# Batch 0 of a Fourier mixing layer: turning rows to partitions with VectorE transposes in SBUF in place of a trip through HBM

## The chip, the cores and the metric

One core of one Trainium2 chip runs the whole kernel. The metric is device time in microseconds (us), lower is better. Engines are named as in the profile: PE is TensorE's matmuls, PEld its weight loads, DVE is VectorE, ACT ScalarE, POOL GpSimd, SP SyncE (it only issues DMAs here). "L291" is a line of the kernel that was profiled, so one statement has different numbers in different kernels.

Ratios below are the mean time of one kernel's fast runs over the mean time of the other's fast runs of the same rounds on the same chip, with a 95% interval. They are therefore not quite the ratio of the medians that stand beside them.

## The reference, cut to what matters

```python
X = np.fft.rfft(x, axis=1)                  # x: 8 x 3008 x 256
y = np.fft.irfft(X * F, n=3008, axis=1)     # F = filt_r + 1j * filt_i
out = (np.maximum(y @ w_gate, 0) * (y @ w_val)) @ w_out    # 24064 rows, 256 -> 1536 -> 256
```

## The kernel before

The transform of length 3008 is done as 94 x 32, all in matmuls:

- **Stage A** transforms along the 94 (`n1`, on the partitions). Its output has the frequency rows on the partitions and the 32 values of `n2` in the free direction.
- **Stage B** needs `n2` on the partitions: it transforms along `n2`, multiplies with the filter, and transforms back.
- **The inverse** along the 94 gives `yT`, and the **main loop** does the gate, value and output matmuls over 47 blocks of 512 rows.

Batch 0 does the first three steps alone, as a prologue. Batch 1's stage A is spread over batch 0's stage B, the later batches over the main loop. Before the change batch 0's data were turned by writing stage A's rows to HBM and reading them back in another order:

```python
Abuf = [dram.tile([NROW * N2, D], BF16, name=f"Abuf{b}") for b in range(B)]
...
def items_a(b):                              # 16 items; 4 of them make a chunk c
    def one(c, j, st):
        ...
        nc.tensor.matmul(psA[0:NROW], WA, XF[c * NC2 // NX2][:, o:o + 512], start=True, stop=True)
        nc.scalar.copy(dst, psA[0:NROW])
        if j == 3:                           # chunk c complete: write it
            eng = nc.scalar if b and c > 1 else nc.sync
            eng.dma_start(_ap(Abuf[b], ...), st["asb"][:NROW])
...
def load_at(b, c):                           # ... and read it with n2 on the partitions
    nc.sync.dma_start(ats[b][c:c + 125:4], _ap(Abuf[b], c * NROW * NC2 * D, [[D, 32], [4 * NC2 * D, NG], [1, D]]))
```

The prologue, cut:

```python
warm(11)                                     # junk matmuls
for i, f in enumerate(items_a(0)): f()       # stage A of batch 0
for c in range(4): load_at(0, c)
... make_back_t, make_back_u (tables), place_filter (copies of the filters), place_nyq
for i in range(14): warm(2)                  # junk matmuls during the trip
load_x(1, nc.sync, ...)                      # x of batch 1
early = items_a(1)
def amid(i):                                 # called in step i of stage B
    if i < 2: warm(6, 256)
    else:
        for _ in range((1, 1, 2, 1, 1)[i - 2]): next(early)()
first_b(amid)                                # stage B of batch 0, six steps
load_d(0, 0, 2)                              # stage B's output goes through HBM too (Dbuf -> dC)
...
load_at(1, 0)
for i, f in enumerate(early):                # the rest of batch 1's stage A
    f()
    if i == 5: load_at(1, 1)
    if i == 7:
        for h in range(2): item_c(0, h)      # first inverse, then the main loop starts
```

## Time and profile before

| | before |
|---|---|
| median of three runs | 894.28 us |
| span of the profiled run | 892.0 us |
| first product of stage B starts (VectorE) | 34.78 us |
| stage B's last output copy ends (ScalarE) | 51.00 us |
| first inverse matmul starts | 57.35 us |
| first value matmul of the main loop starts | 59.59 us |
| longest idle time of TensorE between stage A and the main loop | 2.14 us (32.20 to 34.34) |

Most of the lines from which this comes stand in the prediction below. The four points in time in the middle are the ones to follow: from the last of them on TensorE is full (busy for 825.09 of the 832 us from 60 us on in the kernel before), so what that point moves, the end moves. Two more lines of the kernel before will be compared, the stretches around the start of the main loop (columns: length; busy us of PE, PEld, DVE, ACT, POOL with the number of instructions; granted clock of TensorE; DMA share; GB/s):

```profile
55.00:60.00 5.00, 4.54 (x23) 1.83 (x22) 0.69 (x1) 3.12 (x6) 4.04 (x7) 1.00 1.09 195
60.00:65.00 5.00, 4.64 (x21) 1.94 (x20) 2.70 (x5) 3.20 (x6) 5.00 (x4) 1.00 1.20 272
```

The column to note is the clock, 1.00 in both.

### The profile page before, as it was taken

To read this page: it belongs to the slowest core of one execution; us is meant where nothing else is said; L and a number is where in the kernel's file an instruction comes from. 1 tells how busy PE (TensorE), PEld (TensorE's weight loads), DVE (VectorE), ACT (ScalarE), POOL (GpSimd) and SP (SyncE) were. 2 spreads that over 40 slices of the span, in tenths; PEclk is the share of its full clock that TensorE was granted. 3 is DMA by queue.
4 is the path that set the end of the run, shared out by engine and by line. 5 is a ranking of instruction groups with operands and counts; after the bars stand their busy time and mean duration, and the time that the engine had idled before them with its cause. 6 is when DMAs were issued, how large, how long until landed. Compare 5 with 4: busy or idle time off the path is not lost.

```text
span 892.0 us, 19155 instructions
## 1 busy us (share of the span) xinstructions
PE 875.7 (98%) x7208; PEld 506.8 (57%) x7208; DVE 567.1 (64%) x871; ACT 504.2 (57%) x893; POOL 364.4 (41%) x361
## 2 busy tenths in 40 slices
PE   7899999999999999999999999999999999999997
PEld 2335655566556665566655565556655566666665
DVE  2736776577665766667766677657776577655553
ACT  4675555555655566556555556555655555555553
POOL 4350697038651476316671176802867000000001
PEclk9999999999999999999999999999999999999999
DMA  9997448534456336453376334662446512331111
GB/s 244 305 235 141 143 138 166 119 102 130 120 142 133 116 97 155 130 125 97 96 174 146 86 102 109 175 139 78 116 141 148 121 31 81 76 79 36 37 32 53
DMA packets 114099, 109.18 MB, mean 122 GB/s; under 512 B 20359, under 2 KB 98599, under 8 KB 113366
## 3 DMA queue, kind: packets, MB, share of 16 engines
q1 hardware_dynamic: 90294, 80.10, 34.7%
q0 software_dynamic: 22992, 26.41, 12.3%
q8 instruction: 57, 0.93, 0.5%
q10 hardware_dynamic: 720, 1.45, 0.4%
q14 instruction: 36, 0.29, 0.1%
HBM read 61.93 MB, written 49.81 MB: 125 GB/s over the span
## 4 chain that ended last, share of the span: by engine, by line
PE 93%; DMA 3%; ACT 1%; POOL 1%; issue 1%; DVE 0%; SPq 0%; ACTq 0%; POOLq 0%
PE psV L467 28%; PE psG L467 27%; PE psO L486 27%; PE psF L323 3%; PE psY L451 2%; PE psD L394 2%; PE psX L364 2%; PE psA L276 2%; DMA dC<-Dbuf 1%; DMA Abuf<-asb 1%; DMA at<-Abuf 1%; DMA XF<-in_x_dram 1%; ACT dsb L401 0%; DMA Dbuf<-dsb 0%; SPq L176 0%
## 5 line engine op out<-in xcount | busy, mean ns | idle before, releaser
L472 DVE SCALAR_TENSOR_TENSOR prod<-psG,vsb 128x512 bf16<-128x512 f32 x564 | 389.2, 690 | 263.6 <-ACT vsb L470 258.1
L470 ACT CAST vsb<-psV 128x512 bf16<-128x512 f32 x564 | 331.8, 589 | 263.0 <-PE psV L467 170.9
L467 PE MATMUL psV<-yT,WvT 128*128 128x512 bf16 x1128 | 336.6, 380 | 0.7 <-ACT asb L330 0.4
L486 PE MATMUL psO<-WoT,prod 128*128 128x256 bf16 x2256 | 336.5, 273 | 0.0
L467 PE MATMUL psG<-yT,WgT 128*128 128x512 bf16 x1128 | 335.4, 379 | 0.7 <-ACT dsb L401 0.3
L486 PEld LDWEIGHTS <-prod 128*128 128x128 bf16 x2256 | 220.2, 98 | 143.8
L467 PEld LDWEIGHTS <-WgT 128*128 128x128 bf16 x1128 | 109.9, 97 | 135.9 <-issue 2.5
L467 PEld LDWEIGHTS <-WvT 128*128 128x128 bf16 x1128 | 98.4, 98 | 41.9 <-issue 30.4
L258 POOL CAST scr<-prod 128x8 f32<-128x8 bf16 x24 | 4.5, 189 | 258.3 <-DVE prod L472 258.3
L509 POOL DMA_DIRECT2D out_dram<-osb x5 | 2.6, 536 | 195.9 <-ACT osb L499 195.9
L499 ACT COPY osb<-psO 128x512 f32<-128x512 f32 x92 | 53.9, 586 | 27.6 <-PE psO L486 26.1
L380 DVE TENSOR_TENSOR tt<-psX,Ftr 128x512 bf16<-128x512 f32 x96 | 65.1, 682 | 5.9 <-PE psX L364 5.9
L309 POOL TENSOR_TENSOR fold<-XP 128x1024 f32<-128x1024 f32 x24 | 56.5, 2355 | 20.5 <-PE psF L323 19.2
L380 DVE TENSOR_TENSOR uu<-psX,Fti 128x512 bf16<-128x512 f32 x89 | 60.6, 681 | 0.0
L401 ACT CAST dsb<-psD 128x512 bf16<-128x512 f32 x96 | 51.5, 589 | 12.1 <-PE psD L394 11.8
L296 POOL DMA_DIRECT2D XP<-in_x_dram x96 | 56.7, 596 | 3.2 <-PE psG L467 1.6
L310 POOL TENSOR_TENSOR XP<-XP 128x1024 f32<-128x1024 f32 x24 | 56.4, 2349 | 1.9
L330 ACT CAST asb<-psF 128x512 bf16<-128x512 f32 x48 | 25.8, 589 | 30.5 <-PE psF L323 30.5
L330 DVE CAST asb<-psF 128x512 bf16<-128x512 f32 x48 | 30.9, 686 | 18.6 <-PE psF L323 18.6
L456 ACT CAST yT<-psY 128x512 bf16<-128x512 f32 x47 | 27.5, 586 | 23.8 <-PE psY L451 23.6
L451 PE MATMUL psY<-M,dC 96*128 96x94 bf16 (+18 forms) x604 | 37.7, 199 | 1.4 <-DMA dC<-Dbuf 1.2
L458 DVE CAST yT<-psY 128x512 bf16<-128x512 f32 x47 | 32.0, 681 | 9.8 <-PE psY L451 9.8
(72 smaller groups left out, 493.5 us busy)
## 6 DMA issues: line engine op xcount, KB each, us to landing
at<-Abuf SPq DMA_DIRECT2D x32, 384.0 KB
dC<-Dbuf SPq DMA_DIRECT2D x64, 192.0 KB
XP<-in_x_dram POOLq DMA_DIRECT2D x48, 256.0 KB, 6.1
Dbuf<-dsb SPq DMA_DIRECT2D x23, 512.0 KB
XP<-in_x_dram POOLq DMA_DIRECT2D x96, 96.0 KB, 2.7
Abuf<-asb SPq DMA_DIRECT2D x96, 96.0 KB
out_dram<-osb SPq DMA_DIRECT2D x69, 94.0 KB
XF<-in_x_dram SPq DMA_DIRECT2D x15, 256.0 KB
```

Of the source, the lines that this page charges most:

```text
L296: nc.gpsimd.dma_start(xp[r:r + 24, 0:4:2, :], _ap(x, (b * N1 * N2 + o) * D, [[N2 * D, 24], [47 * N2 * D, 2], [1, 512]]))
L309: tt(t, xp[:, 0:2], xp[:, 2:4], op=ALU.add)
L310: tt(xp[:, 2:4], xp[:, 0:2], xp[:, 2:4], op=ALU.subtract)
L330: copy(asf[:, :, q, :], banks[q])
L380: nc.vector.tensor_tensor(p, psX, filt, op=ALU.mult)
L401: nc.scalar.copy(dsb[:, a, o:o + 2, :], psD[a])
L451: nc.tensor.matmul(psY[:, o:o + w], dCs[b, n2 // 8][:, n2 % 8, h * 128:(h + 1) * 128], M1[:, n1:n1 + w], start=True, stop=True)
L467: nc.tensor.matmul(pt[:, :W], w[:, h, ft * 128:(ft + 1) * 128], yt[:, h, :], start=(h == 0), stop=(h == 1))
L470: nc.scalar.copy(vsb, psV[:, :W])
L472: nc.vector.scalar_tensor_tensor(prod, in0=psG[:, :W], scalar=0.0, in1=vsb, op0=ALU.max, op1=ALU.mult)
L486: nc.tensor.matmul(psO[:, t % 2], prods[ft][:, t * 128:(t + 1) * 128], WoT[:, ft, :], start=(ft == 0), stop=(ft == NFT - 1))
L499: copy(osb[:, t0 % 2:t % 2 + 1], psO[:, t0 % 2:t % 2 + 1])
```

## The change

Its intent is to take the write and the read through HBM off the start of the kernel. Stage A of batch 0 now computes 128 rows in an order of their own, ScalarE writes them as bf16 into `AS`, and two VectorE transposes, to which pairs of bf16 are given as one 4-byte word, turn `AS` into `AT`, which stage B reads. Around this the prologue is rearranged. The diff, cut to its core:

```diff
-    wa = np.zeros((128, NROW))
+    wa = np.zeros((128, 128 + NROW))          # a second set of columns, in the turn's order
...
+    AS = pro.tile([128, NC2, N2 // NC2, D], BF16)
+    AT = pro.tile([128, 32, D], BF16)
...
+    def first_a(i):
+        c, j = divmod(i, 4)
+        psA = matmul_a(c, j, slice(0, 128))
+        nc.scalar.copy(AS[:, 2 * j:2 * j + 2, c, :], psA.rearrange("p (n d) -> p n d", n=2))
+    def turn_a():
+        src = AS.rearrange("p l c d -> p (l c) d").bitcast(FP32).rearrange("p n d -> p d n")
+        dst = AT.bitcast(FP32).rearrange("p k d -> p d k")
+        for h in range(2):
+            cols = slice(h * D // 4, (h + 1) * D // 4)
+            nc.vector.transpose(dst[:, cols, :], src[:, cols, :])
+        ats[0] = AT
...                                            # prologue; the tables now come ahead of stage A
-    for i, f in enumerate(items_a(0)):
-        f()
-    for c in range(4):
-        load_at(0, c)
+    for i in range(16):
+        first_a(i)
...
+    for a in range(2):
+        place_filter(0, a, 0, nc.vector.tensor_copy)
+    turn_a()
+    for i in range(9):                         # was 14, and warm(6)
+        warm(2)
...                                            # upper filter halves by DMA, x of batch 1 behind them
+            place_filter(fi, a, 1, nc.sync.dma_start)
+        load_x(1, nc.sync, cols)
...
     def amid(i):
-        if i < 2:
-            warm(6, 256)
-        else:
-            for _ in range((1, 1, 2, 1, 1)[i - 2]):
-                next(early)()
+        if i == 3:
+            place_nyq()
+        for _ in range((1, 1, 1, 2, 1, 2, 1)[i]):
+            next(early)()
...
     for i, f in enumerate(early):
         f()
-        if i == 5:
+        if i == 2:
             load_at(1, 1)
-        if i == 7:
+        if i == 4:
             for h in range(2):
                 item_c(0, h)
```

So 9 instead of 6 of batch 1's stage-A items lie inside stage B, and 5 instead of 8 between stage B and the first inverse.

More of the change, by code (lines that the diff above doesn't have):

```diff
@@ L57, in _tables @@
         e, j = g % 2, 12 * a + g // 2
-        ra, rm = 4 * j + 2 * e, 48 * e + j
+        rt, ra, rm = 64 * e + j, 128 + 4 * j + 2 * e, 48 * e + j
         f = np.zeros((64, 64))
@@ L63, in _tables @@
         th = 2 * np.pi * (((n1 - 23) * k1) % N1) / N1
-        wa[part, ra] = np.cos(th)
+        wa[part, rt] = wa[part, ra] = np.cos(th)
         if k1 not in (0, 47):
-            wa[part, ra + 1] = -np.sin(th)
+            wa[part, rt + 32] = wa[part, ra + 1] = -np.sin(th)
             m1[rm] = 2.0 * np.cos(th) / S
@@ L152 @@
     pro = prologue.enter_context(tc.tile_pool(name="pro", bufs=1))
-    Abuf = [dram.tile([NROW * N2, D], BF16, name=f"Abuf{b}") for b in range(B)]
+    Abuf = [dram.tile([NROW * N2, D], BF16, name=f"Abuf{b}") if b else None for b in range(B)]
     Dbuf = [dram.tile([NROW * N2, D], BF16, name=f"Dbuf{b}") for b in range(B)]
     XF = [pro.tile([128, NX2 * D], FP32, name=f"XF{c}") for c in range(N2 // NX2)]
-    WA = pro.tile([128, NROW], FP32)
+    WA = pro.tile([128, 128 + NROW], FP32)
+    AS = pro.tile([128, NC2, N2 // NC2, D], BF16)
+    AT = pro.tile([128, 32, D], BF16)
     WF = consts.tile([128, 4, 32], FP32)
@@ L267, in fft_tag, with matmul_a @@
         return turn["tags"][turn["i"] % len(turn["tags"])]
+    def matmul_a(c, j, cols):
+        psA = ps.tile([128, 512], FP32, tag=fft_tag(True), name="psA")
+        o = (c * NC2 % NX2) * D + j * 512
+        nc.tensor.matmul(psA[0:cols.stop - cols.start], WA[:, cols], XF[c * NC2 // NX2][:, o:o + 512],
+                         start=True, stop=True)
+        return psA
+    def first_a(i):
[9 more added lines that the diff above has]
+        ats[0] = AT
     def items_a(b):
@@ L273, in one @@
                 st["asb"] = sb.tile([128, NC2 * D], BF16, tag="asb", bufs=4, name="asb")
-            psA = ps.tile([128, 512], FP32, tag=fft_tag(True), name="psA")
-            o = (c * NC2 % NX2) * D + j * 512
-            nc.tensor.matmul(psA[0:NROW], WA, XF[c * NC2 // NX2][:, o:o + 512],
-                             start=True, stop=True)
-            dst = st["asb"][:NROW, j * 512:(j + 1) * 512]
-            nc.scalar.copy(dst, psA[0:NROW])
+            psA = matmul_a(c, j, slice(128, 128 + NROW))
+            nc.scalar.copy(st["asb"][:NROW, j * 512:(j + 1) * 512], psA[0:NROW])
             if j == 3:
-                eng = nc.scalar if b and c > 1 else nc.sync
+                eng = nc.scalar if c > 1 else nc.sync
                 eng.dma_start(_ap(Abuf[b], c * NROW * NC2 * D, [[NC2 * D, NROW], [1, NC2 * D]]),
@@ L541 @@
         pass
-    warm(11)
-    for i, f in enumerate(items_a(0)):
-        f()
-    for c in range(4):
-        load_at(0, c)
+    warm(8)
     for i in range(3):
         make_back_t(i)
-    warm(6)
-    place_filter(0, 1, 0, nc.scalar.copy)
-    for i in range(3):
-        make_back_u(i)
-    for a, half in ((0, 0), (0, 1), (1, 1)):
-        place_filter(0, a, half, nc.vector.tensor_copy)
-    place_own()
-    for a, half, copy in ((1, 0, nc.scalar.copy), (0, 0, nc.vector.tensor_copy),
-                          (0, 1, nc.vector.tensor_copy), (1, 1, nc.vector.tensor_copy)):
-        place_filter(1, a, half, copy)
-    place_nyq()
-    for i in range(14):
-        warm(2)
-    load_x(1, nc.sync, ((0, 0, 2 * q), (0, 2 * q, 4 * q), (1, 0, 4 * q)))
+    warm(3)
+    for i in range(16):
+        first_a(i)
+        if i == 3:
+            for n in range(3):
+                make_back_u(n)
+    place_own()
+    for a in range(2):
+        place_filter(0, a, 0, nc.vector.tensor_copy)
+    turn_a()
+    for i in range(9):
+        warm(2)
+    place_filter(1, 1, 0, nc.scalar.copy)
+    place_filter(1, 0, 0, nc.vector.tensor_copy)
+    for fi, cols in ((0, ((0, 0, 2 * q), (0, 2 * q, 4 * q))), (1, ((1, 0, 4 * q),))):
+        for a in range(2):
+            place_filter(fi, a, 1, nc.sync.dma_start)
+        load_x(1, nc.sync, cols)
     nc.sync.dma_start(WF, nc.inline_tensor(fold_h, name="dft_fold").ap())
@@ L568, in amid @@
     def amid(i):
-        if i < 2:
-            warm(6, 256)
-        else:
-            for _ in range((1, 1, 2, 1, 1)[i - 2]):
-                next(early)()
-    hold_gpsimd(ats[0][0:32, NG - 1, 0:8])
+        if i == 3:
+            place_nyq()
+        for _ in range((1, 1, 1, 2, 1, 2, 1)[i]):
+            next(early)()
+    hold_gpsimd(AT[0:32, NG - 1, D - 8:])
     load_vg(0, DFF // 2)
@@ L580 @@
     load_d(0, 0, 2)
-    nc.gpsimd.dma_start(pro.tile([1, D], BF16, tag="last", bufs=1, name="last"),
+    nc.gpsimd.dma_start(pro.tile([1, D], BF16, tag="nyq", bufs=2, name="last"),
                         _ap(Dbuf[0], (N2 * NROW - 1) * D, [[D, 1], [1, D]]))
```

## The prediction

> **What bounds the kernel now.** I read the page first (busy shares, then the chain that ended last), then the busy time by stretches of the span, then the chain in order of time over the first 60 us, and last the groups of instructions and the waits of that stretch.
>
> ```profile
> span 892.0 us, 19155 instructions
> PE 875.7 (98%) x7208; PEld 506.8 (57%) x7208; DVE 567.1 (64%) x871; ACT 504.2 (57%) x893; POOL 364.4 (41%) x361
> PE 93%; DMA 3%; ACT 1%; POOL 1%; issue 1%; DVE 0%; SPq 0%; ACTq 0%; POOLq 0%
> ...
> 200.00:400.00 200.00, 200.00 (x1720) 116.89 (x1719) 133.99 (x206) 114.66 (x206) 104.18 (x97) 1.00 0.50 128
> ...
> 30.00:35.00 5.00, 2.86 (x22) 1.25 (x20) 2.44 (x6) 2.00 (x1) 0.33 (x2) 1.00 0.98 317
> ```
>
> The columns of the stretches are length, then busy time of PE, PEld, DVE, ACT, POOL, the granted clock, the DMA share and GB/s. From 60 us on TensorE has work without a gap (200.00 of 200 us): nothing done for batch 0 can shorten that part. It can only start earlier. So the change is worth exactly what it moves the first gate/value matmul of the main loop, at 59.6 us. The head of the chain, in order of time (start, length, what):
>
> ```profile
> 12.82 10.53 PE psA L276 x24
> 23.35 0.02 issue
> 23.37 0.59 ACT asb L279
> 23.96 0.02 issue
> 23.98 5.43 DMA Abuf<-asb
> 29.41 0.02 issue
> 29.42 0.02 SPq L350
> 29.44 0.03 issue
> 29.47 4.78 DMA at<-Abuf
> 34.25 0.09 issue
> 34.34 0.46 PE psX L364 x8
> 34.80 0.67 DVE tt L380
> ...
> 51.03 2.41 DMA Dbuf<-dsb
> ...
> 53.83 3.39 DMA dC<-Dbuf
> 57.21 0.14 issue
> 57.35 0.62 PE psY L451 x12
> ```
>
> The reader is to see a turn of the data through HBM: stage A ends on TensorE at 23.35, ScalarE's last copy at 23.96, then a write of 5.43 us and a read of 4.78 us, and only at 34.34 the first stage-B matmul. That is 10.4 us from copy to matmul in which TensorE does table making and warm-up matmuls on junk. After it comes the stage B of batch 0 (34.80 to 51.03), a second trip through HBM (51.03 to 57.21), and the main loop.
>
> [...]
>
> **The change part by part.**
>
> Stage A itself: the same 16 products of 128 rows by 512 columns, now with 128 instead of 96 output rows. The records of one item are two matmuls, 24 of them in 10.53 us, 0.439 us each; [...] The table of weights grows from 48 to 112 KB and is loaded first: at 241 GB/s (stretch 5 to 10 us) an estimated 0.2 to 0.3 us on the arrival of x, which sets the 12.82. The table making (48 small matmuls, three swaps) moves ahead of and into stage A. Its data (384 and 135 KB on ScalarE's queue) are all moved by 6 us, and TensorE waits for x until 12.82 with only 8 records' work (3.9 us) to do; 0.74 us of small matmuls and 0.9 us of swaps fit. End of stage A's copies: 23.96 + 0.25 = 24.2.
>
> The turn: two VectorE instructions, each 128 partitions x 64 x 32 fp32 words = 2048 elements. The pace is from two rows of groups, VectorE casts from fp32:
>
> ```profile
> L197 DVE CAST I2t<-psI 128x256 bf16<-128x256 f32 x6 | 2.1, 416 | 17.3 <-PE psI L192 17.3
> L458 DVE CAST yT<-psY 128x512 bf16<-128x512 f32 x1 | 0.7, 691 | 9.3 <-PE psY L451 9.3
> L238 DVE COPY Ftr<-Ftr 32x3072 bf16<-32x3072 bf16 x3 | 2.8, 948 | 0.1
> ```
>
> The medians are 414 and 681 ns, so 267 ns for 256 elements, 1.04 ns an element, and 147 ns fixed. 2048 x 1.04 + 147 = 2.28 us each, 4.6 us both (an estimate). Ahead of them VectorE copies two filter halves (2 x 0.95 us); the r filters land at about 22 in the trace before (last issued at 14.41, longest landing 7.5 us) and somewhat earlier without stage A's writes in the way, so these copies are over by 24. The turn ends at 24.2 + 4.6 = 28.8. Stage B's first matmuls need 0.46 us, but VectorE still has one filter copy (0.95) before the first product: product at 29.8 against 34.80 before. Gain 5.0 us. All of it is on the path; of the 10.4 us of DMA about half comes back as VectorE time.
>
> The upper filter halves: before, six VectorE copies and two of ScalarE; now three and one, and four DMAs of 192 KB inside SBUF. They are needed at the earliest at the fourth of six steps of stage B, some 8 us after its start, so they are hidden. ScalarE's 2.75 us copy of the i filter starts when that filter has landed. Before it waited until 29.25; with 0.43, 0.23 and 0.37 MB of stage A's writes gone from the stretches 16 to 25 us, I put it at 27, end 29.8, just in time for the first product with the i filter at 30.4.
>
> Stage B: the warm-up matmuls of steps 0 and 1 become stage-A items of batch 1, and there are 9 items inside it instead of 6. Each is one more ScalarE copy of 0.58 us. ScalarE is what is full there:
>
> ```profile
> 40.00:45.00 5.00, 4.28 (x54) 2.01 (x54) 3.66 (x6) 4.71 (x11) 4.16 (x4) 1.00 1.06 238
> 45.00:50.00 5.00, 5.00 (x64) 2.05 (x63) 2.60 (x5) 4.78 (x11) 1.16 (x1) 1.00 0.86 279
> ```
>
> Followed copy by copy: the two early ones push the first output copy (39.09 before, 4.29 us after the first product) by 0.6 us, later steps carry some 0.25 more, and the third extra one adds 0.58, of which 0.3 fits into ScalarE's gaps. Stage B gets 1.1 us longer.
>
> After stage B: 5 items of batch 1 instead of 8 lie before the first matmul of the inverse. They cover the second trip through HBM, which needs 6.3 us and doesn't get shorter; TensorE then idles about 3 us, at no cost. Two items stay after it, as before. One more 0.38 MB write of batch 1 falls next to the last writes of stage B: 0.4 us (an estimate, a third of the 1.2 us that it takes at 317 GB/s).
>
> Sum: -5.0 + 1.1 + 0.4 = -3.5 us; 894.3 - 3.5 = **890.8 us**.
>
> **The rivals.**
>
> First: the transposes run at half pace because of the 512-byte steps. Then they take 2 x (147 + 4096 x 1.04) = 8.8 us, the start gains 0.8 only, and stage B's extra work makes it 895. [...] Against: the diff cuts the warm-up matmuls ahead of stage B from 34 to 18 (0.22 us each). Before, they end at 32.2, 2.1 us ahead of the first stage-B matmul; now they end at 27.4. Whoever tuned this expected stage B at about 29.5.
>
> Second: the filters become the wait that takes the place of the trip through HBM. The DMA engines are full from 10 to 45 us (share 0.96 and more), and x of batch 1 is now requested at about 22 instead of 30, right among the i filter's packets. If that filter still lands at 29.2, ScalarE's copy ends at 32.0 and the first product with it comes 1.6 us late: 892.4. For it: the saturated DMA. Against: 3 MB less of A's traffic in the same time.
>
> Third: ScalarE or the first item's x doesn't delay stage B at all, since its copies find gaps. Then only the start counts: 889.3 with the 0.4, and 888.9 without.
>
> Fourth: the weights hold the main loop, so an earlier start is hidden. Their first halves are asked for at 34.84 and take up to 11.8 us, far ahead of 59.6; now they are asked for at 29. The second halves are asked for after stage B's last write and shift with it. I see no wait for them in TensorE's list (largest after 24 us: 2.1 for the turned data). This one would make 894; I hardly believe it.
>
> **Range and chances.** 80% goes to 888.8 to 893.8: the lower end is the third rival, the upper end is the second with a slow start of x or some part of the first. About 12% lies above (half pace), the rest below. The most that the removed trip could give is 10.4 us, 1.2%, so faster than 2% (under 876.4) can't come from here, and no part costs the 18 us for slower. Within 2%: 0.98.
>
> **What would show it right or wrong.** Right: two transposes of 2.2 to 2.4 us each starting near 24.2, the first stage-B matmul near 28.9, the first product near 29.8, the last stage-B output copy near 47, the first gate/value matmul near 56, and TensorE full from there as before. Half pace shows as 4.4 us transposes; the second rival as ScalarE's filter copy starting after 28 on a DMA and VectorE or TensorE waiting behind it; the third as a stage B of 16.2 us; the fourth as a TensorE wait for weights after 56. Wrong altogether would be a stage A that ends a microsecond or more later, because the table making ahead of it holds up its first items, or a wait for x of batch 1 in stage B's first steps.

What is cut, with a mark, are general statements on the hardware: a paragraph on transposes, SBUF and DMAs, a clause on stage A, and one ground for the first rival. The sum: it came to -5.0 + 1.1 + 0.4 = -3.5 us, so 890.8. Stage A's wider output counts as zero in it, which was the author's estimate (measured since: in the chains 24 records in 10.55 us with 128 rows, 10.53 with 96). The pace of the transposes was an estimate from two casts, and the "half pace" of the first rival a supposition that no trace showed then.

## More of the kernel before

The rounds ran on different chips, and the kernel before has medians between 893.51 and 895.19 us in them. A fall of the time that is reckoned from one round to another is uncertain by as much; the points in time in the traces are the surer measure.

## The result, and the profile after

The changed kernel is correct and slower: 900.11 us (899.61 to 900.52, 4 runs) against 894.16 us, ratio 1.0068, interval 1.0051 to 1.0086. Within the class "within 2%" that had been given 98%, but outside the range, and of the wrong sign.

| | before | after | difference |
|---|---|---|---|
| first product of stage B starts | 34.78 | 32.48 | -2.30 |
| stage B, first product to end of last output copy | 16.22 | 17.77 | +1.55 |
| second trip through HBM, from there to the first inverse matmul | 6.35 | 10.81 | +4.46 |
| from there to the first value matmul | 2.24 | 4.37 | +2.13 |
| first value matmul starts | 59.59 | 65.43 | +5.84 |

The differences of the first four rows add up to the last one, and the last is nearly the whole difference of the medians, 5.95. The lines of the last row, before and after:

```profile
59.59 0.60 PE L467 MATMUL psV<-yT,WvT 128*128 128x512 bf16 x2
65.43 1.06 PE L488 MATMUL psV<-yT,WvT 128*128 128x512 bf16 x2
```

The four rows can be taken one by one. The chain that ended last, of the changed kernel, in order of time:

```profile
22.59 0.59 ACT AS L283
...
23.35 3.93 issue
27.27 4.19 DVE AT L291
...
50.28 2.42 DMA Dbuf<-dsb
...
53.22 7.80 DMA dC<-Dbuf
...
61.06 1.03 PE psY L472 x12
62.10 3.54 PE psA L275 x4
65.64 0.85 PE psV L488 x2
```

The reader is to see four things. The trip of 10.2 us is gone, but the turn takes its place with 8.3 us (the first transpose is shown as "issue", 23.35 to 27.27, and the second by name). The read of the second trip, `dC<-Dbuf`, takes 7.80 us where it took 3.39. And the same matmuls after it are slow: 12 inverse matmuls 1.03 us instead of 0.62, the first value pair 0.85. The group of the transposes (count, busy us, mean ns of one, idle time before them):

```profile
L291 DVE STREAM_TRANSPOSE AT<-AS 128x2048 f32<-128x2048 f32 x2 | 8.3, 4225 | 2.1 <-ACT AS L283 2.1
```

4.2 us for 2048 words, where 2.28 had been predicted. What TensorE waited for, longest first (total, times, longest), and the stretches of the changed kernel that match the slow places:

```profile
PE psY L472 <- DMA dC<-Dbuf: 7.5, 1, 7.5
PE psX L385 <- DVE AT L291: 5.1, 1, 5.1
```

```profile
30.00:35.00 5.00, 3.48 (x19) 1.16 (x20) 4.58 (x6) 0.60 (x2) 2.37 (x3) 0.50 0.96 314
55.00:60.00 5.00, 0.00 (x0) 0.00 (x0) 0.00 (x0) 0.00 (x0) 1.76 (x3) 0.72 0.99 178
60.00:65.00 5.00, 3.94 (x16) 1.96 (x17) 0.69 (x1) 1.17 (x2) 1.80 (x3) 0.50 1.21 254
```

After each of the two waits the clock column falls to half: 0.50 from 30 to 35 us and from 60 to 65 us, where the kernel before has 1.00. That was nowhere in the prediction.

The theory after this reading has four parts: the transposes are slow because of their 512-byte steps; the idle time of TensorE during the turn costs clock in stage B; batch 1's third stage-A write, which the denser schedule puts 0.35 us ahead of the `dC` reads, holds these reads; and the long wait that follows costs clock again. Rivals: a 4-byte transpose is slow as such; stage B is longer because ScalarE has more to copy; the `dC` reads are slow because of the weights or of the earlier `load_at(1, 1)`; the slow start of the main loop is a matter of data, not of clock.

### The profile page after: what moved, and what is told of

It reads as the page before. It is cut to its first block, busy times and chain, and to the rows that moved or that the text cites. A ratio compares the mean times of both kernels' runs of the same rounds, so it can differ in the third digit from the quotient of the medians.

```text
span 898.4 us, 18964 instructions
## 1 busy us (share of the span) xinstructions
PE 868.5 (97%) x7059; PEld 507.2 (56%) x7180; DVE 573.3 (64%) x870; ACT 501.9 (56%) x892; POOL 365.6 (41%) x361
## 3 DMA queue, kind: packets, MB, share of 16 engines
HBM read 60.42 MB, written 48.23 MB: 121 GB/s over the span
## 4 chain that ended last, share of the span: by engine, by line
PE 85%; DVE 5%; ACT 4%; DMA 3%; issue 2%; SPq 1%; POOL 1%; DVEq 0%; ACTq 0%
PE psG L488 26%; PE psO L507 25%; PE psV L488 24%; DVE prod L493 3%; ACT vsb L491 3%; PE psF L344 3%; PE psD L415 2%; DMA dC<-Dbuf 2%; PE psA L275 2%; PE psX L385 2%; PE psY L472 2%; SPq L178 1%; DVE AT L291 0%; DMA XF<-in_x_dram 0%; POOL uu L399 0%
## 5 line engine op out<-in xcount | busy, mean ns | idle before, releaser
L488 PE MATMUL psG<-yT,WgT 128*128 128x512 bf16 x1107 | 331.0, 379 | 6.7 <-DVE prod L493 0.5
L488 PE MATMUL psV<-yT,WvT 128*128 128x512 bf16 x1030 | 315.9, 380 | 0.5 <-ACT asb L351 0.5
```

The costliest lines, as they stand in the source:

```text
L488: nc.tensor.matmul(pt[:, :W], w[:, h, ft * 128:(ft + 1) * 128], yt[:, h, :], start=(h == 0), stop=(h == 1))
```

## The experiments

Twelve kernels ran. All edits are to the changed kernel unless said otherwise. This is where each has its four points (us), with the median, the kernel before in the same rounds, and the ratio:

| kernel | first product | stage B ends | first inverse | first value | median | before | ratio (95%) |
|---|---|---|---|---|---|---|---|
| e1_fill_turn | 32.22 | 49.31 | 60.01 | 64.13 | 899.07 | 895.19 | 1.0045 (1.0025 to 1.0065) |
| e2_fill_trip | 32.63 | 50.43 | 61.38 | 63.63 | 897.24 | 895.19 | 1.0028 (1.0012 to 1.0043) |
| e3_late_write | 32.37 | 49.64 | 56.21 | 60.55 | 894.67 | 895.19 | 1.0003 (0.9987 to 1.0018) |
| e5_fewer_items | 32.57 | 47.96 | 54.52 | 56.76 | 892.28 | 893.51 | 0.9987 (0.9971 to 1.0004) |
| c1_three | 32.48 | 49.56 | 56.22 | 58.46 | 894.22 | 893.51 | 1.0008 (0.9990 to 1.0025) |
| c4_few_fill | 32.84 | 48.23 | 54.63 | 56.88 | 891.95 | 894.23 | 0.9969 (0.9954 to 0.9983) |
| c2_sliced | 28.36 | 44.30 | 50.78 | 53.02 | 888.19 | 893.51 | 0.9940 (0.9920 to 0.9961) |
| c3_no_x_wait | 27.65 | 43.42 | 49.63 | 51.88 | 888.19 | 894.25 | 0.9939 (0.9924 to 0.9955) |

### The clock after the turn: e1_fill_turn

```diff
     turn_a()
-    for i in range(9):
+    for i in range(17):
         warm(2)
```

> The changed kernel with 34 instead of 18 junk matmuls during the turn, so that TensorE doesn't idle 5.1 us before stage B. If the idle gap is what halved the granted clock (0.50 at 30 to 35 us), the clock stays near 1.0 there, the first two stage-A items inside stage B take 1.1 instead of 2.0 us, stage B from its first product to its last output copy goes from 17.8 to some 16.8 us, and the time falls by about 1 us to 899. If stage B is longer only because of the extra items on ScalarE, it stays at 17.8 and the time at 900.1.

The idle time before stage B shrank from 5.08 to 1.62 us and the clock stayed up, as the stretch of this kernel shows:

```profile
30.00:35.00 5.00, 3.48 (x33) 1.15 (x34) 4.94 (x7) 0.86 (x2) 2.56 (x4) 1.00 0.94 316
```

Stage B took 17.09 us instead of 17.77, the first value matmul came 1.3 us earlier, and the median is 1 us lower. So in these two traces the clock costs stage B 0.7 us; the other 0.9 of its 1.55 are not clock, and both theories get a part. The 0.7 is not a fixed price. In e3_late_write the same gap (5.11 us) was followed by half clock until about 34.8 us, where the changed kernel has it until about 36.7, and stage B took 17.27 us.

### The clock after the second trip: e2_fill_trip

```diff
         if i == 4:
+            for _ in range(16):
+                warm(2)
             for h in range(2):
                 item_c(0, h)
```

> The changed kernel with 32 junk matmuls in the gap of 7.5 us that TensorE idles before the first inverse matmul. If that gap costs clock (0.63 at 60 to 70 us), the stretch from the first inverse matmul to the first value matmul goes from 4.6 back to 2.4 us and the time falls by 2.5 to 3 us, to 897.3. If the slow start of the main loop is a matter of DMA or weights, the time stays at 900.1.

In the chain of this kernel the inverse (0.62 in the kernel before) and the two items after it (1.78, as in the kernel before) are back to their old lengths:

```profile
61.38 0.64 PE psY L472 x12
```

From the first inverse to the first value matmul it is 2.25 us instead of 4.37, though the `dC` data land as late as before the edit. The slow start of the main loop is the clock: it is 1.00 from 60 to 65 us here, 0.50 in the changed kernel. The median fell by 2.9 us, as expected, the profiled run by 2.3 and the first value matmul by 1.8.

### The late read of the second trip: e3_late_write and e5_fewer_items

```diff
-                eng = nc.scalar if c > 1 else nc.sync
+                eng = nc.scalar if c > 2 else nc.sync      # e3_late_write: the third write queues behind the reads
```

> The changed kernel with the third write of batch 1's stage A put on the queue behind the reads of the second trip instead of on ScalarE's queue ahead of them. If that write is what held the reads (2 us in which their queue moved 0.02 MB), the reads land 3.5 to 4 us after their first issue instead of 7.8, the gap of TensorE shrinks to about 4 us, and the time falls by 3.5 to 5 us, to 895 to 896.6. If the reads are slow because of the weights or of the re-read of batch 1's rows, they still take over 7 us and the time stays at 900.

DMA traffic from 53 to 55 us by queue (packets, MB, share of the 16 engines). First the changed kernel, where q10 is ScalarE's queue with the write and q1 SyncE's with the reads, then e3_late_write:

```profile
q10 hardware_dynamic: 95, 0.36, 78.8%
q1 hardware_dynamic: 36, 0.02, 3.0%
```

```profile
q1 hardware_dynamic: 840, 0.42, 84.3%
```

In the changed kernel the write has the engines for most of these 2 us and the reads move 0.02 MB; the weights then come on (queue q0) while the reads are still at it. Without the write ahead of them the reads land after 3.35 us instead of 7.80, though `load_at(1, 1)` is issued at 55.60, no later than in the changed kernel (56.34), so that rival falls.

The write itself accounts for about 1 us of this, as a finer cut of the same traces shows. Where no write stands ahead of them, the reads move their first packets some 0.9 us after their first issue (issued at 53.45 and moving from about 54.4 in the kernel before, 52.35 and 53.3 in e3_late_write). In the changed kernel it is 1.9 us (52.85 and 54.8): from 53.75 to 54.75 us the write's queue moved 0.18 MB and the queue of the reads nothing. The rest comes from what the reads meet when they are late. In e3_late_write they have 84.3% of the engines' time from 53 to 55 us and land at 56.07. In the changed kernel they have moved 0.22 MB by 56 us, against 0.57 in e3_late_write, and from 56 to 61 us the weights take 66% of the engines' time. The weights alone are not the cause, since e3_late_write has them as well; how much they add to the 1 us was not tried in a run of its own.

From the chain of e3_late_write:

```profile
52.72 3.35 DMA dC<-Dbuf
56.21 1.01 PE psY L472 x12
```

The median fell by 5.4 us and the first value matmul by 4.9. The second line holds a surprise: TensorE had waited only 3.26 us (52.95 to 56.21), and the inverse is still slow, 1.01 us; the clock was 0.50 from 56 to 62 us.

The same write can be moved in time instead of to another queue:

```diff
-        for _ in range((1, 1, 1, 2, 1, 2, 1)[i]):
+        for _ in range((1, 1, 1, 1, 1, 1, 1)[i]):      # e5_fewer_items; load_at(1, 1) at i == 4, item_c at i == 6
```

> The changed kernel with 7 instead of 9 stage-A items of batch 1 inside stage B (one in each step), so 7 instead of 5 before the first inverse matmul. ScalarE's queue keeps the third write. If it is the time of that write, not its queue, that held the reads of the second trip, they land 3.4 us after their last predecessor again, as before. TensorE's gap shrinks from 7.5 to about 2 us, so no clock is lost after it, and stage B loses about 0.6 us of ScalarE's copies. Time 892 to 893.5. If the queue matters and not the time, the reads still take over 7 us and the time is above 898.

The reads were in time with the write still on ScalarE's queue; the first inverse matmul of this kernel, with its wait in brackets:

```profile
54.52 0.62 PE L472 MATMUL psY<-M,dC 96*128 96x94 bf16 x12 [1.53 <-DMA dC<-Dbuf]
```

The write is issued at 51.92 here, 1.4 us behind the first read (50.55). So it is the moment of the write, not its queue. This edit does more: TensorE waits 1.53 us only, no clock is lost there (1.00 from 55 to 60 us), and stage B shrinks to 15.39 us, less than before the change (16.22). It has no step with two items, the changed kernel has two, the kernel before has one. 17.09 (two, clock repaired), 16.22 (one), 15.39 (none): about 0.85 us for each doubled step, which is the length of one item on TensorE (0.88 us: 24 records in 10.54 us are 12 items). The chain of e1_fill_turn runs through both items of each doubled step:

```profile
39.29 1.89 PE psA L275 x4
44.12 1.90 PE psA L275 x4
```

By the same comparison the items in the first two steps, which took the place of junk matmuls, cost nothing; no run tests them alone.

### All repairs: c1_three and c4_few_fill

c1_three is e1_fill_turn and e3_late_write with 16 junk matmuls before the inverse.

> The changed kernel with all three repairs: junk matmuls in both gaps (34 during the turn, 16 before the inverse) and the late write. If the three causes are all that the change gave back, the gains add: 1.0 for the clock in stage B, 3.9 to 5.4 for the write with its gap, about 2 for the clock after the gap: 892.3 to 893.3. Then it beats the kernel before by 1.5 to 2.5 us, about what the start of stage B gained (2.3). If something else in the change costs too, it stays above 894.5.

A miss, if a small one. The profiled run does what was expected (first value matmul at 58.46, 1.1 us ahead of the kernel before, and 892.85 us), but its four runs spread from 892.85 to 896.18, and the median is not below the kernel before. With one microsecond at stake this number of runs cannot tell. In its trace the second trip (6.66 us) and the way to the first value matmul (2.24) are back where they were before the change, and 0.86 us of stage B, the doubled step, is what remains.

c4_few_fill is e5_fewer_items and e1_fill_turn together.

> e5_fewer_items with the junk matmuls of e1_fill_turn: the whole change with its transposes as they are, 7 items inside stage B and no idle gap of TensorE over 2 us. If the two repairs add, stage B ends 0.7 us earlier than in e5_fewer_items, the first value matmul comes at about 56 against 59.6 before, and the time is 891 to 892, a gain over the kernel before that is clear of noise. If stage B is bound by ScalarE whatever the clock, it stays at 892.3.

891.95 us, a gain clear of noise over the kernel before, but for half of the stated reason: stage B took 15.39 us with the clock kept up (1.00 from 30 to 35 us), as in e5_fewer_items without (0.69). With no doubled step the half clock at its beginning (until about 35 us in e5_fewer_items) is not on the path. The first value matmul comes at 56.88, no earlier than in e5_fewer_items (56.76), and the intervals of the two ratios overlap: nothing shows that the junk matmuls added to what the 7 items gave.

### The pace of the transposes: t1_contig and t2_half

Both: same instructions, same number of words, other access patterns. Their outputs are wrong, which doesn't matter for the times.

```diff
-        for h in range(2):
-            cols = slice(h * D // 4, (h + 1) * D // 4)
-            nc.vector.transpose(dst[:, cols, :], src[:, cols, :])
+        # t1_contig: contiguous to contiguous, then 512-byte steps to contiguous
+        nc.vector.transpose(flat_d[:, 0:2048], flat_s[:, 0:2048])
+        nc.vector.transpose(flat_d[:, 2048:4096].rearrange("p (d k) -> p d k", k=32), src[:, 64:128, :])
+        # t2_half: contiguous to 512-byte steps, then runs of 16 bytes to 512-byte steps
+        nc.vector.transpose(dst[:, 0:64, :], flat_s[:, 0:2048].rearrange("p (d n) -> p d n", n=32))
+        nc.vector.transpose(dst[:, 64:128, :].rearrange("p d (l c) -> p d l c", c=4),
+                            flat_s[:, 2048:4096].rearrange("p (l d c) -> p d l c", l=8, c=4))
```

> Wrong result on purpose. The changed kernel with other access patterns in its two transposes, the same 2048 words each: the first reads and writes contiguously, the second reads in steps of 512 bytes and writes contiguously. If the stride sets the pace, the first takes 2.3 us and the second 2.3 (if only the writing counts) or 4.2 (if the reading counts). If a 4-byte word goes at half pace as such, both take 4.2 us.

> Wrong result on purpose. The other two access patterns of a transpose of 2048 words: the first reads contiguously and writes in steps of 512 bytes, the second reads runs of 16 bytes (four words) and writes in steps of 512 bytes. With 2.31 us for both sides contiguous, 3.65 for the reading side alone in steps and 4.2 for both, three cases are open: the writing side alone costs nothing (first 2.3), costs by itself (first 3 to 3.7), or the two sides overlap and the slower counts (first near 3.6). [...]

The transposes' groups, first of t1_contig (L291 contiguous on both sides, L292 reading in steps), then of t2_half (L290 writing in steps, L291 reading 16-byte runs and writing in steps):

```profile
L292 DVE STREAM_TRANSPOSE AT<-AS 128x2048 f32<-128x2048 f32 x1 | 3.6, 3649 | 0.0
L291 DVE STREAM_TRANSPOSE AT<-AS 128x2048 f32<-128x2048 f32 x1 | 2.3, 2311 | 0.6 <-ACT AS L283 0.6
```

```profile
L290 DVE STREAM_TRANSPOSE AT<-AS 128x2048 f32<-128x2048 f32 x1 | 3.7, 3716 | 1.3 <-ACT AS L283 1.3
L291 DVE STREAM_TRANSPOSE AT<-AS 128x2048 f32<-128x2048 f32 x1 | 3.6, 3635 | 0.0
```

Contiguous, the transpose has the predicted pace: 2.31 us against 2.28. So a 4-byte word is not slow as such. Steps of 512 bytes on either side alone make it 3.65 to 3.72, on both sides 4.2. By the word, fixed part included, that is 1.13 ns contiguous, 1.78 reading in steps, 1.81 writing in steps and 2.06 both (2311, 3649, 3716 and 4225 ns over 2048 words). Reading in runs of 16 bytes is as cheap as reading contiguously (3.64 beside 3.72 with the same writing); shorter runs were not tried. Each pattern was run once.

### The filter copies alone: p1_filters_only and p2_filters_nyq

These are edits to the kernel before.

```diff
-    for a, half in ((0, 0), (0, 1), (1, 1)):
-        place_filter(0, a, half, nc.vector.tensor_copy)
+    place_filter(0, 0, 0, nc.vector.tensor_copy)
+    for a in range(2):
+        place_filter(0, a, 1, nc.sync.dma_start)
...                                             # the same for the i filter
-    place_nyq()                                # p2_filters_nyq only: moved into amid(3)
```

> The kernel before with one part of the change alone: the upper halves of both filters copied by four DMAs inside SBUF behind the reads of the turned data, instead of four VectorE copies. These copies lie beside other work in both forms, so the theory that they are hidden says 893 to 895, as before, with the first product of stage B near 34.8 still. If the four DMAs delay x of batch 1 behind them (2.4 us of issue), TensorE waits for x in stage B and it is 895 to 897.

899.64 us, ratio 1.0061 (1.0048 to 1.0074), 5.4 us slower: neither theory. One cause is the order on VectorE. The row copies of `place_nyq`, which overlap the last filter group, stood ahead of the first product, and now waited for the DMAs:

```profile
37.91 0.22 DVE L242 COPY Fti<-nyq 1x256 bf16<-1x256 bf16 x1 [1.26 <-DMA Fti<-Fti]
```

The change moves these copies into stage B.

> p1_filters_only with the row copies of the last filter group moved to the fourth step of stage B, as the whole change has them: in p1_filters_only they stood ahead of the first product on VectorE and held it until the last filter DMA had landed (37.86). If that order is the cause, the first product starts again when the turned data are there, at 35 to 36 us, and the time is 893.5 to 896 (the rest being x of batch 1 behind the four DMAs). If the DMAs themselves are too slow for stage B, it stays above 898.

897.15 us, ratio 1.0027 (1.0010 to 1.0043). The first product starts at 37.10, not at 35 to 36, and the median is 1 us above the range that was given: the order explains about half of it. The rest begins with the read of the turned rows, 4.78 us in the kernel before and 6.63 here. That the filter copies beside it are what slows it is argued, not shown. Because of the late read TensorE idled 4.27 us here (3.81 in p1_filters_only), and the clock was 0.57 from 36 to 40 us (0.70 there), so a part of both losses may be clock again, which no run tried alone. The DMAs are thus not free in the kernel before (p2_filters_nyq has them and is 3.0 us slower). In the changed kernel there is no such read, and no VectorE instruction in stage B waits for a filter DMA.

### A version that beats both: c2_sliced and c3_no_x_wait

Stage A cannot be turned before all its 32 columns of `n2` are there. But the second half of x can go through stage A by slices of `d` instead of by `n2`; then each slice is complete after two items and VectorE turns it while TensorE makes the next.

```diff
     def first_a(i):
         c, j = divmod(i, 4)
+        if i < 8:
...                                             # as before
+        s, c = divmod(i - 8, 2)
+        ds = slice(64 * s, 64 * s + 64)
+        rhs = XF[1].rearrange("p (n d) -> p n d", d=D)[:, 8 * c:8 * c + 8, ds]
+        nc.tensor.matmul(psA, WA[:, 0:128], rhs, start=True, stop=True)
+        nc.scalar.copy(AS[:, :, 2 + c, ds], psA.rearrange("p (l d) -> p l d", d=64))
+        if c == 1:
+            turn_slice(s)                       # one transpose of 128 x 1024 words
...                                             # e5_fewer_items, and:
-        place_filter(0, a, 0, nc.vector.tensor_copy)
+        place_filter(0, a, 0, nc.sync.dma_start)
```

> A version meant to beat both: 7 items as in e5_fewer_items; the second half of x goes through stage A in four slices of 64 columns, so that VectorE turns a slice while TensorE makes the next one; the lower halves of the r filter are copied by DMA too, off VectorE. Four transposes of 1024 words at 2.05 ns and 0.1 us each, 2.2 us, the first from about 17.9: end near 26.7 instead of 31.5. First product near 27.7 instead of 32.5, so 4.8 us ahead of e5_fewer_items: 887 to 889. If the i filter's arrival (25.3 and a copy of 2.75) is the next bound, the first product with it waits until 28 to 29.5 and it is 889 to 891.

888.19 us, inside the range: 5.3 us below the kernel before, 11.9 below the changed one (of another round). VectorE of this kernel:

```profile
18.84 8.51 DVE L300 STREAM_TRANSPOSE AT<-AS 128x1024 f32<-128x1024 f32 x4 [4.88 <-ACT AS L291]
```

The transposes are as slow as ever (8.51 us for the four), but they start at 18.84 instead of 23.21, and the first product starts at 28.36. Against e5_fewer_items of the same rounds this is 4.2 us at the first product and 4.1 in the median, for the slices and the filter DMAs together.

c3_no_x_wait replaces the item in stage B's first step, where TensorE waited 1.69 us for x, by junk matmuls, and has one item more after stage B.

> c2_sliced with junk matmuls instead of the stage-A item in the first step of stage B, where TensorE waited 1.69 us for x of batch 1, and so 6 items inside and 8 after. The second step's product can start about 0.7 us earlier (VectorE is then the limit), and ScalarE has one copy less: 886.5 to 888 where c2_sliced is 888.2. If another engine takes up the slack it stays at 888.

The points came 0.7 us (first product) and 1.1 us (first value matmul) earlier. The 0.7 are not the edit's: the first transpose already starts at 18.14 instead of 18.84, ahead of anything that was edited. That leaves 0.4 for the edit. The median did not move, and six runs spread from 886.42 to 891.32. It is within the noise of c2_sliced.

## Why the prediction was wrong, point by point

The frame held: the worth of the change is what it moves the first value matmul (59.59 to 65.43, and 5.95 us in the time). The terms of the sum did not.

- **The turn (predicted -5.0 for the first product, measured -2.30).** The term "2048 x 1.04 + 147 = 2.28 us each" was mis-sized: 4.2 us each. The number is right for contiguous sides (2.31) and was taken from casts that step contiguously. The first rival, given about 12%, is what happened to the turn, though its total of 895 us was not reached either. The turn took 8.26 us where 4.6 had been predicted, 3.7 more. An earlier end of stage A's copies (23.18, predicted 24.2) took back 1.0, and the first product came 2.7 us later than predicted. Some of that 1.0 is scatter, see below.
- **Stage B (+1.1, measured +1.55).** The size was near, the reason was not. It was argued from ScalarE's copies of three extra items. The runs show 0.7 us of lost clock and about 0.85 us for one more step with two items, and by comparison nothing for the items in the first two steps. That the size came near is luck.
- **The second trip ("doesn't get shorter", and 0.4 us for a write beside it; measured +4.46).** This is the term that was worst mis-sized. The prediction saw that three more items move into stage B, counted their copies, and one more write, but did not ask when the following chunk's write would now be issued: at 52.50, 0.35 us ahead of the reads that the main loop waits for. In the kernel before it was issued at 55.82, 2.4 us behind the first of them (53.45). e3_late_write moves this one write and gets 4.2 us of the trip back (6.57 instead of 10.81).
- **"TensorE then idles about 3 us, at no cost" (not in the sum; measured +2.13).** This step failed outright. The idle time was 7.5 us, but even 3.26 us (e3_late_write) brought the half clock, and e2_fill_trip shows the whole 2.13 gone with junk matmuls in the gap. The same holds for the cut from 34 to 18 junk matmuls, which the prediction read as evidence of a fast turn: it left 5.08 us of idle time, and the clock was 0.50 behind it. In one look even 2.30 us of idle time (t2_half) was followed by a clock of 0.50 from 30 to 33 us, while it was 1.00 behind the 2.14 us of the kernel before.
- **The rivals.** The second (filters as the bound) did not come true here, though it is next in line: in t1_contig, with a faster turn, the first product with the i filter waited 0.6 us for ScalarE's filter copy. The fourth (weights hold the main loop) did not show.
- **The chances.** All within 2% was right. The range's upper end, 893.8, left no room for two terms failing at once. A slip in the third rival (894.3 - 5.0 is 889.3 without the 0.4, and 889.7 with it) changes nothing.

Stage A itself ended 0.8 us earlier than before, with x landing earlier (TensorE's run of twelve items starts at 12.01, before at 12.82). This need not be the change: in p1_filters_only, whose code is the same as the kernel before up to there, its last copy starts at 22.43 instead of 23.37, and in the kernels with the changed stage A it starts between 22.34 and 23.46. So the gain of 2.30 us at the first product holds up to 0.8 us of scatter between executions. It stays open why the DMA engines served the write first.

## What to carry to other kernels

A schedule that hides work in another stage also moves when that work's outputs are written; follow each moved transfer to the place where it is now issued, and ask which read that others wait for comes right behind it. Idle time of TensorE had a price here where what followed was on the path (2.13 us behind the gap of 7.50): after an edit moves or lengthens a wait, look at the granted clock behind every gap. The runs don't fix a length that is safe: in p1_filters_only the clock was 0.68 from 40 to 45 us, where no single wait was over 1 us. Take a duration from a row with the same access pattern, not only the same element count (2.31 and 4.2 us here for the same 2048 words); where a slow operation cannot be made fast, cutting it into slices that start earlier may give more.
